# Attention, gating and mixing on one core: bank choice by longest free, and a fixed order for the first pair of heads

## The chip, the cores and the metric

The kernel runs on one core of one Trainium2 chip. The metric is the device time of one execution in microseconds (us); lower is better. A core has TensorE (PE, with its weight loads as PEld), VectorE (DVE), ScalarE (ACT), GpSimd (POOL) and SyncE (SP). SP and ACT both issue DMAs; their queues are written SPq and ACTq.

## The reference

Three blocks follow each other: attention over 4 x 12 heads of 448 tokens and 64 dimensions, a gated block with a spatial mix, and a token and channel mixer. Only the first touches the change:

```python
def rmsnorm(x, g):
    rms = np.sqrt(np.mean(x * x, axis=-1, keepdims=True) + 1e-06)
    return x / rms * g
q_n, k_n = (rmsnorm(q, g_q), rmsnorm(k, g_k))
scores = scale * np.matmul(q_n, k_n.transpose(0, 1, 3, 2))
scores = scores - np.max(scores, axis=-1, keepdims=True)
attn = np.exp(scores)
attn = attn / (np.sum(attn, axis=-1, keepdims=True) + 1e-09)
return np.matmul(attn, v).astype(np.float32)
```

The gated block computes relu(x w_in), splits it into u and v, normalises v, mixes it over tokens and multiplies; its weights, w_in among them, come as 8-byte floats and are converted word by word on the chip. The mixer is two more two-layer blocks, the last of which ("up" with products h2ps, "down" with products o_ps) is done as seven products of half-size blocks.

## The kernel before, in words

**Pairs.** Heads are worked in 24 pairs. `Attention.load` (line 634) brings q and k of a pair into one tile `raw` (two buffers); for pair 0 k's four pieces are issued by ACT, everything else by SP. `norms` (666) squares q and k on ACT, sums on DVE and calls `rsqrt` (605): Ln and Exp on ACT, with five small operations on POOL. `scale` (689) multiplies `raw` by the roots, on DVE for pair 0 and on POOL after it. `transposed` (699) turns q and k through PE into PSUM tiles `tp`, and copies them out as `qt` and `kt` (name `whole`); k's copy multiplies by the gain product `gg`. `scores` (728) makes the scores of one chunk of 112 tokens for both heads (tiles `sc`), their maxima on DVE (`nm`), and the exponentials on ACT (`e`). `turned` turns the exponentials (`et`), `values` multiplies by v (`av`).

**Start.** `start` (837) loads pair 0 and the gains, lets PE do 26 warm-up matmuls on zeros (`WARM`, 897), loads pair 1, and does norms, scaling and transposes of pair 0, and the norms of pair 1. After it, `slot` (863) yields one pair at a time, and other work is merged between: `prepare_v` (905) converts half of w_in through `convert` (540), whose first step is an Abs on ACT, then four bit operations on DVE (tile `word`), a copy on ACT and a difference on POOL (`wv`).

**Order.** Nothing is issued as the program is written. Every call goes into a `Plan` (150): each operation has a modelled cost (`estimate`, 217), dependencies and a weight. `place` (267) is a list scheduler: it keeps a clock for each engine, and always gives the engine that is free first its ready operation of least weight. Operations of POOL with SBUF operands and some of DVE's share a modelled port. `issue` (383) runs it forwards and backwards for eight rounds, the backward run giving the weights, and keeps the shortest plan. So each engine's instruction order is the plan's order of start times, and at run time an engine waits in that order.

**PSUM.** A PSUM tile is of kind sc, tp or mm. `Banks` (129) has eight banks, of which 4, 2 and 2 are reserved for the kinds. When `place` reaches the first operation of a tile, it picks one of the banks that are free at the planned time; before, the one that became free last:

```python
for k in ks:
    n = max(x for x in free_banks if x[0] <= t)
    free_banks.remove(n)
    bank[k] = n[1]
```

A bank's next writer waits at run time for the real last reader of the tile that had it.

Of the kernel before, what the change touches and what calls it, by code (L numbers as in the profile page):

```python
# [12 lines left out]
F32 = mybir.dt.float32  # L13
F32R = mybir.dt.float32r
U32 = mybir.dt.uint32
AF = mybir.ActivationFunctionType
# [133 lines left out]
class Plan:  # L150
# [116 lines left out]
    def place(self, before, after, lag, weight, tiles=None):  # L267
# [21 lines left out]
        while placed < len(ops):  # L289
# [35 lines left out]
            if tiles is not None and i in opens:  # L325
                ks = opens[i]
                kind = ks[0].psum
                spare = len(free_banks) - sum(max(0, n - held[x]) for x, n in Banks.OWN.items() if x != kind)
                if spare < len(ks):
                    blocked.append(i)  # L330
                    continue
                free_banks.sort()
                at = free_banks[len(ks) - 1][0]
                if at > t:
                    heapq.heappush(due[e], (at, i))
                    continue
                for k in ks:
                    n = max(x for x in free_banks if x[0] <= t)
                    free_banks.remove(n)
                    bank[k] = n[1]  # L340
                held[kind] += len(ks)
# [130 lines left out]
def attention_moe_mixer(  # L472
# [15 lines left out]
    C = 4  # L488
# [50 lines left out]

    def convert(pool, tag, bufs, raw, rows, n, dst_hi, dst_lo, dims=None, at=None):  # L540

        if f64:
            r = raw.rearrange("p (n w) -> p n w", w=2)
            a = pool.tile([rows, n], U32, tag=tag, bufs=bufs, name="word") if at is None else at
            low, high = r[:, :, 0], r[:, :, 1]
            nc.scalar.activation(a.bitcast(F32), high.bitcast(F32), AF.Abs)
            nc.vector.tensor_scalar(a.bitcast(F32), a.bitcast(F32), least, most, ALU.max, ALU.min)
            nc.vector.tensor_scalar(a, a, 5, 2, ALU.logical_shift_left, ALU.logical_shift_right)
            nc.vector.scalar_tensor_tensor(a, high, 0xC0000000, a, ALU.bitwise_and, ALU.bitwise_or)
            nc.vector.scalar_tensor_tensor(a, low, 29, a, ALU.logical_shift_right, ALU.bitwise_or)  # L550
        else:
            a = raw
# [51 lines left out]

    def rsqrt(pool, src, n, w, mul, tag, bufs=2, on=None):

# [3 lines left out]
        z = pool.tile([P, w], F32, tag=tag + "z", bufs=bufs, name=tag + "z")  # L610
        on.tensor_scalar(a[:n], src, mul, 1e-6, ALU.mult, ALU.add)
        nc.scalar.activation(y[:n], a[:n], AF.Ln)
        nc.scalar.activation(y[:n], y[:n], AF.Exp, scale=-0.5)
# [10 lines left out]
    class Attention:  # L624
# [9 lines left out]
        def load(self, i):  # L634
# [3 lines left out]
            t = self.p.tile([T, 2, C, 2, D], F32, tag="raw", bufs=2, name="raw")  # L638
            for r in range(2):
                nc.sync.dma_start(  # L640
                    out=t[:, 0, :, r], in_=q[b, 2 * j + r].rearrange("(c p) d -> p c d", p=T))
            on = nc.sync if i else nc.scalar
            on.dma_start(out=t[:, 1, :, 0], in_=k[b, 2 * j].rearrange("(c p) d -> p c d", p=T))

            src = k[b, 2 * j + 1]
            on.dma_start(out=t[:R, 1, 0, 1], in_=src[LAST:])
            on.dma_start(out=t[R:, 1, 0, 1], in_=src[:T - R])
            on.dma_start(
                out=t[:, 1, 1:, 1], in_=src[T - R:LAST].rearrange("(c p) d -> p c d", p=T))
            self.raw[i] = t  # L650
            if i == 2:
# [13 lines left out]

        def norms(self, i):
            if not 0 <= i < NP:
# [3 lines left out]
            ss = p.tile([P, n], F32, tag="ss", bufs=3, name="ss")  # L671
            self.r[i] = []
            for h in (slice(0, n // 2), slice(n // 2, n)):
                if i == 0 and h.start:
                    sq = p.tile([T, 2, S], F32, tag="e", bufs=EB, name="e").rearrange("p r s -> p (r s)")
                    sq = sq[:, :n // 2 * D].rearrange("p (n d) -> p n d", d=D)
                else:
                    sq = p.tile([T, n // 2, D], F32, tag="sq", bufs=1, name="sq")
                nc.scalar.activation(sq, raw[:, h], AF.Square)
                nc.vector.reduce_sum(ss[:T, h], sq, axis=AX.X)  # L680
                if i == 0:
                    self.r[i].append(rsqrt(
                        p, ss[:T, h], T, n // 2, 1.0 / D, f"r{h.start}", bufs=1,
                        on=nc.gpsimd))
            if i:
                r = rsqrt(p, ss[:T], T, n, 1.0 / D, "r", bufs=3, on=nc.gpsimd)
                self.r[i] = [r[:, :n // 2], r[:, n // 2:]]
# [10 lines left out]

        def transposed(self, i, a):
            if not 0 <= i < NP:  # L700
# [6 lines left out]
            if i < WHOLE:  # L707
                to = self.qt if a == 0 else self.kt
                t = to[i] = self.p.tile([P, S], F32, tag="qt" if a == 0 else "kt", name="whole")
                if i == 0 and a == 0:  # L710
                    nc.vector.tensor_copy(t, tpf)
                else:
                    nc.scalar.activation(t, tpf, AF.Copy, scale=1.0 if a == 0 else self.gg[:, 0:1])
                if a:
                    self.raw.pop(i), self.r.pop(i)
            elif a == 0:
# [11 lines left out]
        def scores(self, i, *cs):  # L728
# [108 lines left out]
        def start(self):  # L837
            self.load(0)
            g = self.p.tile([P, 2], F32, tag="g", bufs=1, name="g")
            for r in range(2):  # L840
                nc.sync.dma_start(out=g[r * D:(r + 1) * D, 0:1], in_=g_q.unsqueeze(1))
                nc.sync.dma_start(out=g[r * D:(r + 1) * D, 1:2], in_=g_k.unsqueeze(1))
            self.gg = self.p.tile([P, 1], F32, tag="gg", bufs=1, name="gg")
# [8 lines left out]
            tp = psum.tile([P, 512], "tp", "warm")  # L852
            zeros = self.rests[0].rearrange("p r d -> p (r d)")
            for _ in range(WARM):
                nc.tensor.matmul(tp[:, :P], zeros, zeros, start=True, stop=True)
# [40 lines left out]
    SLOT = 8  # L896
    WARM = 26
    TWO = 99
# [6 lines left out]
    def prepare_v(mp):  # L905
# [5 lines left out]
        for j in range(KD):  # L911

            wait = [op for _, op in at.third.writers] if j > 1 else ()
            raw = weights(mp, "vn", 4, wdram(w_in)[j * P:(j + 1) * P, DU * W:], P, (DU,), wait)
            convert(mp, "vr", 2, raw, P, DU, wv[:, HI, j], wv[:, LO, j])
            yield
# [575 lines left out]
```

## Time and profile before

| | |
|---|---|
| median of 3 runs | 887.33 us (885.97 to 889.61) |
| profiled execution | 887.2 us, its span 885.0 us |
| mean granted clock of PE | 0.995 |
| instructions | 15472 |
| DMA | 152.27 MB, mean 172 GB/s |

The span is what the trace covers; the 2.2 us beside it lie around it. Busy times are the union of an engine's instructions; DMA issues and waits count as idle. All times below count from the span's start. Nearly every instruction shows line 424, the planner's issuing line, so the groups are told apart by the tiles' names.

### The profile page before, as it was taken

What the parts mean: (1) busy time and instruction counts of PE and PEld (TensorE: products, weight loads), DVE (VectorE), ACT (ScalarE), POOL (GpSimd) and SP (SyncE); (2) the same over time, 40 slices, a digit from 0 to 9 for tenths busy, and PEclk for the clock granted to TensorE, in tenths of its full rate; (3) what the DMA queues carried; (4) which work ended last, traced back from release to release, by engine and by line L of the source; (5) the groups of instructions that cost most, each with busy time, mean ns of one, the idle gap of its engine ahead of it and who ended that gap; (6) DMA issues with size and microseconds to landing.
All of it is one profiled execution on the core that took longest, in us unless ns stands there. A gap on an engine that the chain in (4) does not pass through costs nothing.

```text
span 885.0 us, 15472 instructions
## 1 busy us (share of the span) xinstructions
PE 865.1 (98%) x5018; PEld 718.2 (81%) x5018; DVE 681.0 (77%) x1333; ACT 537.1 (61%) x1278; POOL 412.4 (47%) x541
## 2 busy tenths in 40 slices
PE   7999999999999999999999999999999999999998
PEld 5444567678777787776889999998989999999998
DVE  5799798987777767866366567889889886998973
ACT  5999988778867867866453356555325654343331
POOL 3555655786666646574234123224324108514560
PEclk8999999999999999999999999999999999999999
DMA  6555665566644575344687678776554745661441
GB/s 153 138 148 172 198 185 149 161 183 211 182 131 127 152 216 169 103 128 127 225 252 236 195 227 268 220 245 202 161 160 138 227 125 170 197 188 54 143 152 63
DMA packets 153263, 152.27 MB, mean 172 GB/s; under 512 B 77152, under 2 KB 136352, under 8 KB 153184
## 3 DMA queue, kind: packets, MB, share of 16 engines
q1 hardware_dynamic: 152224, 151.06, 57.2%
q8 instruction: 40, 0.66, 0.3%
q10 hardware_dynamic: 960, 0.23, 0.1%
q14 instruction: 39, 0.32, 0.1%
HBM read 112.44 MB, written 38.80 MB: 171 GB/s over the span
## 4 chain that ended last, share of the span: by engine, by line
PE 79%; DVE 8%; ACT 4%; issue 3%; DMA 3%; POOL 2%; SPq 1%; DVEq 0%; POOLq 0%; ACTq 0%
PE h2ps L424 15%; PE o_ps L424 15%; PE tp L424 9%; PE av L424 7%; PE sc L424 7%; PE vps L424 7%; PE xps L424 6%; PE ups L424 6%; PE sps L424 4%; PE h1ps L424 2%; PE u_ps L424 2%; DVE word L424 1%; DVE c L424 1%; DVE op L424 1%; DVE w L424 1%
## 5 line engine op out<-in xcount | busy, mean ns | idle before, releaser
L424 PE MATMUL h2ps<-op,w 128*128 128x448 f32 x756 | 155.5, 367 | 2.0 <-DVE c L424 2.0
L424 PE MATMUL o_ps<-w,op 128*128 128x384 f32 x882 | 153.6, 334 | 1.6 <-DVE u L424 1.6
L424 PEld LDWEIGHTS o_ps<-w,op 128*128 128x128 f32 x882 | 152.8, 188 | 2.3 <-ACT op L424 1.5
L424 PEld LDWEIGHTS h2ps<-op,w 128*128 128x128 f32 x756 | 141.3, 188 | 14.7 <-DVE c L424 3.7
L424 ACT ACTIVATE e<-sc,nm 112x448 f32<-112x448 f32 x192 | 122.5, 654 | 22.6 <-DVE nm L424 22.3
L424 DVE TENSOR_REDUCE nm<-sc 112x1 f32<-112x448 f32 x192 | 109.4, 614 | 19.6 <-PE sc L424 19.0
L424 POOL TENSOR_TENSOR src<-src 128x384 f32<-128x384 f32 x48 | 61.1, 1283 | 76.5 <-DMA src<-c_d 55.2
L424 ACT ACTIVATE op<-c 128x768 fp32r<-128x768 f32 x49 | 41.5, 847 | 85.5 <-PE o_ps L424 81.9
L424 PEld LDWEIGHTS tp<-ident,e 112*128 112x128 f32 x672 | 72.3, 140 | 24.3 <-ACT et L424 7.2
L424 POOL TENSOR_SCALAR e<-e,sums 112x448 f32<-112x448 f32 x112 | 73.8, 676 | 36.9 <-DVE sums L424 21.2
L424 PE MATMUL tp<-ident,e 112*128 112x112 f32 x672 | 87.1, 262 | 1.9 <-ACT over L424 1.5
L424 ACT ACTIVATE et<-tp 128x448 f32<-128x448 f32 x144 | 71.2, 527 | 18.2 <-PE tp L424 15.6
L424 DVE TENSOR_SCALAR word<-word 128x256 f32<-128x256 f32 (+5 forms) x132 | 57.9, 448 | 24.5 <-ACT word L424 23.4
L424 POOL TENSOR_TENSOR u<-u,o 128x384 f32<-128x384 f32 x28 | 40.3, 1457 | 69.2 <-ACT o L424 38.9
L424 DVE SCALAR_TENSOR_TENSOR word<-raw,word 128x256 uint32<-128x256 uint32 (+2 forms) x132 | 70.7, 541 | 1.3
L424 PE MATMUL ups<-xp,wu 128*128 128x448 f32 x288 | 67.8, 375 | 0.4 <-ACT et L424 0.4
L424 DVE TENSOR_TENSOR op<-c,op 128x768 fp32r<-128x768 f32 x49 | 58.1, 1185 | 10.3 <-ACT op L424 10.3
L424 PE MATMUL av<-et,v 128*64 128x448 f32 x288 | 61.2, 550 | 0.0
L424 DVE TENSOR_TENSOR c<-c,h2ps 128x448 f32<-128x448 f32 x84 | 50.1, 614 | 12.1 <-PE h2ps L424 11.9
L424 PE MATMUL vps<-wv,xp 128*128 128x512 f32 x216 | 59.3, 408 | 0.0
L424 PE MATMUL xps<-wo,g 128*128 128x384 f32 x288 | 58.2, 345 | 0.0
L424 PEld LDWEIGHTS ups<-xp,wu 128*128 128x128 f32 x288 | 52.2, 188 | 5.5 <-issue 1.0
(141 smaller groups left out, 1650.9 us busy)
## 6 DMA issues: line engine op xcount, KB each, us to landing
src<-c_d SPq DMA_DIRECT2D x132, 192.0 KB, 3.1
wu<-wu_d SPq DMA_DIRECT2D x16, 768.0 KB, 4.6
wo<-wo_d SPq DMA_DIRECT2D x16, 768.0 KB, 5.1
raw<-in_moe_w_ch_dram SPq DMA_DIRECT2D x36, 256.0 KB, 3.3
raw<-in_moe_w_ch_dram SPq DMA_DIRECT2D x24, 384.0 KB, 3.6
raw<-in_q_dram SPq DMA_DIRECT2D x48, 112.0 KB, 2.9
u<-u_d SPq DMA_DIRECT2D x28, 192.0 KB, 3.9
out_dram<-u SPq DMA_DIRECT2D x28, 192.0 KB, 1.9
```

The costliest lines, as they stand in the source:

```text
L424: getattr(getattr(self.nc, op.engine), fn)(*args, **kwargs)
```

## The change

It does five things. The bank taken is the one that has been free for longest. Pair 0's loads put k ahead of q: k's two large pieces and then q on SP, k's two small pieces and the gains on ACT. A new `first` takes the place of norms, scaling and transposes for pair 0: k is squared on ACT and its root done with DVE, k alone is scaled, q is squared on POOL and transposed unscaled, its copy is ACT's, and its root comes after k's copy. The exponentials of pair 0 take q's root as their scale, and POOL multiplies their maxima by it. The squares of pair 1 wait for k's scaling, and the first two conversions of w_in wait for the second function of q's root. The warm-up has 16 matmuls, and one more ahead of k's transposes.

```diff
-                    n = max(x for x in free_banks if x[0] <= t)
+                    n = min(x for x in free_banks if x[0] <= t)
...
-    def convert(pool, tag, bufs, raw, rows, n, dst_hi, dst_lo, dims=None, at=None):
+    def convert(pool, tag, bufs, raw, rows, n, dst_hi, dst_lo, dims=None, at=None, wait=()):
...
+            a.tile.after = list(a.tile.after) + list(wait)
             nc.scalar.activation(a.bitcast(F32), high.bitcast(F32), AF.Abs)
...
         on.tensor_scalar(a[:n], src, mul, 1e-6, ALU.mult, ALU.add)
+        y.tile.after = list(y.tile.after) + list(wait)
         nc.scalar.activation(y[:n], a[:n], AF.Ln)
...
+            both = nc.sync if i else nc.scalar
...
+            if i:
+                load_q(0, nc.sync)
+                load_q(1, nc.sync)
+            nc.sync.dma_start(out=t[:, 1, :, 0], in_=k[b, 2 * j].rearrange("(c p) d -> p c d", p=T))
...
+            both.dma_start(out=t[:R, 1, 0, 1], in_=src[LAST:])
+            both.dma_start(out=t[R:, 1, 0, 1], in_=src[:T - R])
+            nc.sync.dma_start(
                 out=t[:, 1, 1:, 1], in_=src[T - R:LAST].rearrange("(c p) d -> p c d", p=T))
+            if not i:
+                load_q(0, nc.sync)
+                load_q(1, nc.sync)
...
+                sq.tile.after = list(sq.tile.after) + list(wait)
                 nc.scalar.activation(sq, raw[:, h], AF.Square)
...
+        def first(self):
+            p, n = self.p, 2 * C
+            raw = self.raw[0].rearrange("p a c r d -> p a (c r) d")
+            self.r[0] = [None, None]
+
+            def squares(a, on):
+                sq = p.tile([T, 2, S], F32, tag="e", bufs=EB, name="e").rearrange("p r s -> p (r s)")
+                sq = sq[:, :n * D].rearrange("p (n d) -> p n d", d=D)
+                if on is nc.scalar:
+                    on.activation(sq, raw[:, a], AF.Square)
+                else:
+                    on.tensor_tensor(sq, raw[:, a], raw[:, a], op=ALU.mult)
+                return sq
+
+            def root(a, on, sq, behind=(), copied=()):
+                ss = p.tile([P, n], F32, tag=f"ss{a}", bufs=1, name="ss")
+                ss.tile.after = list(behind)
+                nc.vector.reduce_sum(ss[:T], sq, axis=AX.X)
+                self.r[0][a] = rsqrt(p, ss[:T], T, n, 1.0 / D, f"r{a}", bufs=1, on=on, wait=copied)
+                return nc.ops[-5]
+
+            sk = squares(1, nc.scalar)
+            sq = squares(0, nc.gpsimd)
+            known = root(1, nc.vector, sk)
+            self.scale(0)
+            scaled = nc.ops[-1]
+            self.scaled, self.known = scaled, known
+            self.transposed(0, 0, [known])
+            self.warm(WARM2, [op for _, op in self.qt[0].tile.writers])
+            self.transposed(0, 1)
+            return root(0, nc.gpsimd, sq, [scaled], [op for _, op in self.kt[0].tile.writers])
...
-            for a in range(2):
+            for a in range(2) if i else (1,):
                 on = nc.gpsimd if i else nc.vector
...
-                if i == 0 and a == 0:
-                    nc.vector.tensor_copy(t, tpf)
-                else:
-                    nc.scalar.activation(t, tpf, AF.Copy, scale=1.0 if a == 0 else self.gg[:, 0:1])
+                t.tile.after = list(t.tile.after) + list(wait)
+                nc.scalar.activation(t, tpf, AF.Copy, scale=1.0 if a == 0 else self.gg[:, 0:1])
...
+                roots = None
+                if i == 0:
+                    roots = self.r[0][0][:T]
+                    greatest, nm = nm, p.tile([P, 2], F32, tag="nm", bufs=4, name="nm")
+                    for r in range(2):
+                        at = 2 * c + r
+                        nc.gpsimd.tensor_tensor(
+                            nm[:T, r:r + 1], greatest[:T, r:r + 1], roots[:, at:at + 1], op=ALU.mult)
                 for r in range(2):
                     at = 2 * c + r
                     nc.scalar.activation(
-                        e[:, r], scs[c][r], AF.Exp, bias=nm[:T, r:r + 1], scale=1.0, accum_out=sums[:T, at:at + 1])
+                        e[:, r], scs[c][r], AF.Exp, bias=nm[:T, r:r + 1],
+                        scale=1.0 if i else roots[:, at:at + 1], accum_out=sums[:T, at:at + 1])
...
-                nc.sync.dma_start(out=g[r * D:(r + 1) * D, 0:1], in_=g_q.unsqueeze(1))
-                nc.sync.dma_start(out=g[r * D:(r + 1) * D, 1:2], in_=g_k.unsqueeze(1))
+                nc.scalar.dma_start(out=g[r * D:(r + 1) * D, 0:1], in_=g_q.unsqueeze(1))
+                nc.scalar.dma_start(out=g[r * D:(r + 1) * D, 1:2], in_=g_k.unsqueeze(1))
...
             self.load(1)
-            self.norms(0)
-            self.scale(0)
-            self.transposed(0, 0)
-            self.transposed(0, 1)
-            self.norms(1)
+            self.rooted = self.first()
+            self.norms(1, [self.scaled])
...
-    WARM = 26
+    WARM, WARM2 = 16, 1
...
+            behind = [] if wait else [at.rooted]
+            convert(mp, "vr", 2, raw, P, DU, wv[:, HI, j], wv[:, LO, j], wait=behind)
```

## Rows read from the trace of the kernel before

**Rows 1.** The page's busy times: engine, us (share of the span), instructions.
```profile
PE 865.1 (98%) x5018; PEld 718.2 (81%) x5018; DVE 681.0 (77%) x1333; ACT 537.1 (61%) x1278; POOL 412.4 (47%) x541
```
**Rows 2.** Stages: start:end length, busy us (instructions) per engine; PEclk granted, DMA share, GB/s.
```profile
0.73:14.47 13.74, 9.65 (x60) 9.03 (x60) 5.24 (x10) 6.04 (x13) 6.23 (x21) 0.96 0.71 169
14.47:20.20 5.73, 5.72 (x16) 2.50 (x18) 4.99 (x9) 3.72 (x11) 0.34 (x1) 0.50 0.68 173
20.20:90.00 69.80, 65.95 (x406) 33.74 (x403) 61.17 (x135) 69.09 (x196) 39.66 (x63) 1.00 0.55 152
90.00:523.50 433.50, 429.80 (x2617) 335.00 (x2616) 314.45 (x755) 295.26 (x785) 236.61 (x356) 1.00 0.60 176
523.50:548.60 25.10, 24.98 (x157) 24.07 (x156) 17.77 (x30) 16.91 (x34) 8.60 (x6) 1.00 0.84 250
548.60:882.00 333.40, 328.99 (x1768) 313.87 (x1768) 277.22 (x398) 146.11 (x244) 120.81 (x92) 1.00 0.54 166
```
**Rows 3.** The chain of waits in the head: start us, us, what.
```profile
7.80 5.41 DMA raw<-in_moe_w_in_dram
...
13.80 0.63 ACT whole L424
```
**Rows 4.** ACT's timeline: start us, us, operation, [idle before, released by].
```profile
6.03 0.63 ACT L424 ACTIVATE e<-raw 112x512 f32<-112x512 f32 x1 [1.42 <-DMA raw<-in_k_dram]
...
7.94 0.21 ACT L424 ACTIVATE r8y<-r8y 112x8 f32<-112x8 f32 x1
...
13.23 0.66 ACT L424 ACTIVATE word<-raw 128x512 f32<-128x512 f32 x1 [1.74 <-DMA raw<-in_moe_w_in_dram]
...
17.00 0.63 ACT L424 ACTIVATE e<-sc,nm 112x448 f32<-112x448 f32 x1 [1.64 <-DVE nm L424]
```
**Rows 5.** PE's timeline: k's transposes of pair 0, and scores at full clock.
```profile
10.99 0.60 PE L424 MATMUL tp<-ident,raw 112*128 112x112 f32 x4 [0.38 <-DVE gg L424]
...
22.85 1.01 PE L424 MATMUL sc<-whole 64*112 64x448 f32 x4
```
**Rows 6.** Timeline of the two issuing queues.
```profile
0.73 0.92 SPq L424 DMA_DIRECT2D raw<-in_q_dram  x2
...
3.38 0.33 ACTq L424 DMA_DIRECT2D raw<-in_k_dram  x1
```
**Rows 7.** DMA issues to 4.5 us: transfer, queue, count, size each, median us to landing.
```profile
raw<-in_k_dram ACTq DMA_DIRECT2D x1, 84.0 KB, 3.0
```
**Rows 8.** Tile views: durations in ns, min/median/max, first and last start in us, forms.
```profile
L424 SPq DMA_DIRECT2D g<-in_g_q_dram x2: 576/585/594, 1.7 to 6.5; - x2
...
L424 DVE TENSOR_TENSOR lrz<-lry x16: 147/153/691, 120.3 to 463.7; 128x1 f32<-128x1 f32 x16
```
**Rows 9.** Timeline of DVE and POOL.
```profile
6.69 0.69 DVE L424 TENSOR_REDUCE ss<-e 112x8 f32<-112x512 f32 x1 [1.37 <-ACT e L424]
...
9.95 0.20 POOL L424 TENSOR_TENSOR r8y<-r8y,r8z 112x8 f32<-112x8 f32 x1
...
10.25 0.68 DVE L424 TENSOR_TENSOR raw<-raw,r8y 112x512 f32<-112x512 f32 x1
...
12.77 2.04 POOL L424 TENSOR_TENSOR raw<-raw,ry 112x512 f32<-112x512 f32 x2
...
13.93 1.62 DVE L424 TENSOR_SCALAR word<-word 128x512 f32<-128x512 f32 x2 [2.40 <-ACT word L424]
...
16.34 1.16 DVE L424 TENSOR_REDUCE nm<-sc 112x1 f32<-112x448 f32 x2
...
18.91 0.42 DVE L424 TENSOR_SCALAR word<-word 128x512 f32<-128x512 f32 x1
...
28.39 1.26 POOL L424 TENSOR_TENSOR wv<-word,wv 128x512 fp32r<-128x512 f32 x1 [1.19 <-ACT wv L424]
```
**Rows 10.** Who PE waited for: us in total, times, longest us.
```profile
PE h2ps L424 <- DVE c L424: 2.0, 3, 0.7
...
PE o_ps L424 <- DVE u L424: 1.6, 2, 1.2
```

More of the change, by code (lines that the diff above doesn't have):

```diff
@@ L603, in mm_tile, with rsqrt @@
         return psum.tile([P, 512], "mm", name)
-    def rsqrt(pool, src, n, w, mul, tag, bufs=2, on=None):
+    def rsqrt(pool, src, n, w, mul, tag, bufs=2, on=None, wait=()):
         on = on or nc.vector
@@ L638, in load, with load_q @@
             t = self.p.tile([T, 2, C, 2, D], F32, tag="raw", bufs=2, name="raw")
-            for r in range(2):
-                nc.sync.dma_start(
+            both = nc.sync if i else nc.scalar
+            def load_q(r, on):
+                on.dma_start(
                     out=t[:, 0, :, r], in_=q[b, 2 * j + r].rearrange("(c p) d -> p c d", p=T))
-            on = nc.sync if i else nc.scalar
-            on.dma_start(out=t[:, 1, :, 0], in_=k[b, 2 * j].rearrange("(c p) d -> p c d", p=T))
+            if i:
+                load_q(0, nc.sync)
+                load_q(1, nc.sync)
+            nc.sync.dma_start(out=t[:, 1, :, 0], in_=k[b, 2 * j].rearrange("(c p) d -> p c d", p=T))
             src = k[b, 2 * j + 1]
-            on.dma_start(out=t[:R, 1, 0, 1], in_=src[LAST:])
-            on.dma_start(out=t[R:, 1, 0, 1], in_=src[:T - R])
-            on.dma_start(
+            both.dma_start(out=t[:R, 1, 0, 1], in_=src[LAST:])
+            both.dma_start(out=t[R:, 1, 0, 1], in_=src[:T - R])
+            nc.sync.dma_start(
                 out=t[:, 1, 1:, 1], in_=src[T - R:LAST].rearrange("(c p) d -> p c d", p=T))
+            if not i:
+                load_q(0, nc.sync)
+                load_q(1, nc.sync)
             self.raw[i] = t
@@ L664, in load_v, with norms @@
             self.v32[i] = t, rest
-        def norms(self, i):
+        def norms(self, i, wait=()):
             if not 0 <= i < NP:
@@ L671, in norms @@
             ss = p.tile([P, n], F32, tag="ss", bufs=3, name="ss")
-            self.r[i] = []
             for h in (slice(0, n // 2), slice(n // 2, n)):
-                if i == 0 and h.start:
-                    sq = p.tile([T, 2, S], F32, tag="e", bufs=EB, name="e").rearrange("p r s -> p (r s)")
-                    sq = sq[:, :n // 2 * D].rearrange("p (n d) -> p n d", d=D)
-                else:
-                    sq = p.tile([T, n // 2, D], F32, tag="sq", bufs=1, name="sq")
+                sq = p.tile([T, n // 2, D], F32, tag="sq", bufs=1, name="sq")
@@ L679, in norms @@
+                sq.tile.after = list(sq.tile.after) + list(wait)
                 nc.scalar.activation(sq, raw[:, h], AF.Square)
                 nc.vector.reduce_sum(ss[:T, h], sq, axis=AX.X)
[L681 to L687, printed above, removed]
+            r = rsqrt(p, ss[:T], T, n, 1.0 / D, "r", bufs=3, on=nc.gpsimd)
@@ new lines, in norms @@
+            self.r[i] = [r[:, :n // 2], r[:, n // 2:]]
+        def first(self):
[26 more added lines that the diff above has]
+            return root(0, nc.gpsimd, sq, [scaled], [op for _, op in self.kt[0].tile.writers])
@@ L689, in scale, with warm @@
+        def warm(self, n, wait=()):
+            tp = psum.tile([P, 512], "tp", "warm")
+            tp.tile.after = list(wait)
+            zeros = self.rests[0].rearrange("p r d -> p (r d)")
+            for _ in range(n):
+                nc.tensor.matmul(tp[:, :P], zeros, zeros, start=True, stop=True)
         def scale(self, i):
@@ L697, in scale, with transposed @@
                 on.tensor_tensor(raw, raw, roots.unsqueeze(2).to_broadcast([T, 2 * C, D]), op=ALU.mult)
-        def transposed(self, i, a):
+        def transposed(self, i, a, wait=()):
             if not 0 <= i < NP:
@@ L709, in transposed @@
                 t = to[i] = self.p.tile([P, S], F32, tag="qt" if a == 0 else "kt", name="whole")
-                if i == 0 and a == 0:
-                    nc.vector.tensor_copy(t, tpf)
-                else:
-                    nc.scalar.activation(t, tpf, AF.Copy, scale=1.0 if a == 0 else self.gg[:, 0:1])
+                t.tile.after = list(t.tile.after) + list(wait)
+                nc.scalar.activation(t, tpf, AF.Copy, scale=1.0 if a == 0 else self.gg[:, 0:1])
                 if a:
-                    self.raw.pop(i), self.r.pop(i)
+                    self.raw.pop(i)
+                    if i:
+                        self.r.pop(i)
             elif a == 0:
@@ L851, in start @@
                 self.rests.append(t)
[L852 to L855, printed above, removed]
+            self.warm(WARM)
             self.load(1)
-            self.norms(0)
-            self.scale(0)
-            self.transposed(0, 0)
-            self.transposed(0, 1)
-            self.norms(1)
+            self.rooted = self.first()
+            self.norms(1, [self.scaled])
         def slot(self, s):
@@ L914, in prepare_v @@
             raw = weights(mp, "vn", 4, wdram(w_in)[j * P:(j + 1) * P, DU * W:], P, (DU,), wait)
-            convert(mp, "vr", 2, raw, P, DU, wv[:, HI, j], wv[:, LO, j])
+            behind = [] if wait else [at.rooted]
+            convert(mp, "vr", 2, raw, P, DU, wv[:, HI, j], wv[:, LO, j], wait=behind)
             yield
```

## The prediction

> **What bounds the kernel now.** I read the page's busy shares first [rows 1]: PE is busy 98% of the span, so the time is PE's work plus the time in which PE has none. The table by stage [rows 2] says where that is. Of the 13.74 us ahead of the first scores PE is busy 9.65, and almost all of that is the warm-up, which computes nothing. From 14.47 to 20.20 PE is full, at a granted clock of 0.50, which is 1.2 GHz. From 20.2 to 90 ACT is busy 69.09 of 69.80 us and PE 65.95: here ACT leads. After that PE leads: 3.7 us without matmuls from 90 to 523.5, 0.1 in the next stage, 4.4 from 548.6 to 882. So two things can be won: the head, which delays ACT's full stretch and everything behind it one for one, and single PE waits, about 8 us in all behind 90.
>
> The chain of waits through the head [rows 3] runs over a load of w_in that lands 5.41 us after its issue at 7.80, and then over a copy of pair 0's k on ACT at 13.80. ACT's timeline [rows 4] shows why a weight load stands there: the conversion of w_in's first word sits ahead of the k copy in ACT's order and starts at 13.23, held by that load, although k's transposes were done at 11.59 [rows 5]. Scores start at 14.47, the first exponential at 17.00.
>
> **The change part by part.**
>
> *k's arrival.* Before, ACT squares k at 6.03, on k's landing; a last piece was issued on ACT's queue only at 3.38 [rows 4, 6]. Now k's two large pieces are SP's first issues, at 0.73 and about 1.19 (0.92 for two [rows 6]); 3.0 to land [rows 7] gives 4.2. The two small pieces and the four gain vectors are six issues on ACT's queue ahead of the square, 0.585 each [rows 8]: 0.77 + 3.5 = 4.3. Some issue may also be held, as the one at 3.38 seems to have been. I take 4.5, ends 4.2 and 5.2. That is 1.5 earlier.
>
> *k's root.* From the square's start to the end of the sum took 1.35 (6.03 to 6.69 + 0.69), and from there to the root's end, 9.95 + 0.20 on POOL, 2.77 [rows 4, 9]. Five POOL operations of 0.20 and two functions of 0.21 are 1.42 of that; the rest, seven hand-overs of 0.19, was lengthened by POOL doing both roots in turn. On DVE the five operations are 0.15 each [rows 8], the functions stay, and hand-overs of 0.1 (an estimate, half of before) make 1.8 in all. That puts the root at 4.5 + 1.35 + 1.8 = 7.65.
>
> But q's squares move to POOL. q is SP's third and fourth issue, at about 2.1, landing at 5.1; a two-operand POOL operation of 512 elements takes 1.26, so POOL reads until 6.4, while DVE is ready for the root at 5.85. The timeline shows what such a meeting does: two DVE operations took 1.62 beside POOL's scaling of 12.77 to 14.81, one alone 0.42 [rows 9]. I add 0.45, root at 8.1; ends 0 and 1.26. The Trainium skill ("SBUF — State Buffer", section "Who interferes with whom") has the same: whichever of the two engines issues first holds the shared pair of ports for its whole instruction and the other is blocked. By that rule the full 1.26 is lost when q lands just ahead of the root, and the head gains 0.8 less than I count; the trace agrees that DVE was stretched until POOL ended.
>
> *To the scores.* Scaling to transposes 0.74 (10.25 to 10.99 [rows 5, 9]), transposes 0.60, k copy 0.63 [rows 3, 5]: scores at 8.1 + 2.0 = 10.1 instead of 14.47, 4.35 earlier. q's copy, now ACT's (0.63 like k's), lies in the hole in which DVE does the root. The second pair's squares now wait for the scaling; behind them in ACT's order stands the k copy, and one square (0.63) just fits into the 1.34 of scaling and transposes. Without those holes each costs its length.
>
> *q's root, behind the scores.* Its sum waits for the scaling and takes 0.69, to 9.5; its two functions wait for the k copy, to 10.6; POOL's four operations at about 0.3 end at 11.8. Behind the sum on DVE stand the maxima: two heads' scores 1.01 at full clock [rows 5], one reduce 0.58 (1.16 for two [rows 9]), so 11.7; POOL's product 0.2 and a hand-over: first exponential at 12.1 against 17.00, 4.9 earlier. The eight POOL products are 0.2 each and hidden behind ACT's exponentials (0.63 each) once the stream runs; without that cover, 1.6.
>
> *w_in.* Its conversion now waits for q's root, but the planner may still put it ahead of the first exponentials. SP issues four gain vectors less (4 x 0.585) and two k pieces more (0.92): 1.4 earlier, so the word lands at 11.8. If ACT does its 0.66 first, the exponential starts at 12.5, 4.5 earlier. If DVE's word operations also stand ahead of the maxima (1.62 in before, and a hand-over), it starts at about 13.9, 3.1 earlier. I take **4.0 us** for the head, between the two and nearer to the first, as the trace shows the stall on ACT; ends 1.8 (the word lands no earlier than 13.21, and DVE waits for it too) and 5.7 (the 4.9, and 0.8 if PE keeps full clock).
>
> On that clock: PE had nothing from 11.59 on and was granted half clock behind it [rows 2, 5]. The new head has ten warm-up matmuls less and shorter holes; which of the two clocks the first scores get, no row tells, and half costs no more than before.
>
> Also moved: pair 2's load waits on SP for a buffer that k's transposes free, 2.1 earlier, and stands behind w_in as before.
>
> *Banks.* Taking the bank free for longest changes no planned start, since every candidate is free in the plan; it changes only how late the real reader may be. That excludes a loss but for noise. In the dense products PE waits three times, 2.0 us, for DVE's evictions of h2ps, and twice, 1.6, for those of o_ps [rows 10]; neither is data of the next product. I count these **3.6 us** as gone; what is late next is the next operand, made by the same DVE. Ends: 0, if they turn up there, and 5.9 (half of the other 4.5 behind 90 as well).
>
> **Sum.** 885.0 - 4.0 - 3.6 = 877.4 of span. The profiled execution took 887.2 for 885.0, 0.13 under the median of the runs, 887.33. So 877.4 + 2.2 + 0.1 = **879.7**.
>
> **The rivals.** About 0.5%, 4.4 us, is what can be told from no change: faster is under 882.9, slower over 891.8.
>
> *The banks do nothing*: the waits come back as waits for DVE's operands. For it: DVE is busy 277 of 333 us there, so it is DVE that is late. Against it: the waits are few and single, so DVE catches up. 883.3, the same by a hair.
>
> *w_in still holds the head*: ACT's and DVE's order puts the word ahead of the first exponentials, and SP's queue gains nothing. For it: ACT's stall of before is this very one. Against it: fewer issues on SP ahead of the load. Head 1.8: 881.9; with the banks doing nothing as well, 885.5. The change then doesn't do what it says: scores early, exponentials not.
>
> *The redrawn order uncovers the token stage* (slower). A new head makes the planner draw the whole order anew. From 523.5 to 548.6 PE is kept busy 24.98 of 25.10 us by what work is left over while tokens come in by DMA. If half that cover is spent earlier PE idles 12.5: 892.2. From 7.6 us of lost cover on the gain is gone. For it: the cover is the plan's doing, and the plan goes by modelled costs. Against it: the plan is picked for its length, and the stage shows almost no idle now.
>
> **How the numbers follow.** Forecast (head 3.1 to 5.7, banks 1.5 to 5.9): 0.53. Banks nothing: 0.19. w_in holds: 0.13, and both: 0.06. Token stage uncovered: 0.07. Beyond the good ends: 0.02. Faster takes the forecast less its weak corner (0.05), most of the w_in case (0.12) and the last: 0.62. Slower is the token stage, 0.07; the rest is 0.31. Low end: 885.0 - 5.7 - 5.9 + 2.3 = 875.7, set to 875.0 for what the redrawn order adds; high end 886.5, over both small cases together.
>
> **What the next profile would show.** Right: k's square near 4.5, scores near 10, the first exponential between 12 and 14, ACT full from some 4 us earlier, no PE wait of h2ps or o_ps on an eviction, a span near 877. Wrong: scores early, but ACT idle ahead of a word conversion; DVE's root stretched by more than 0.45 beside POOL's squares; new PE waits on op in the dense products; idle slices of PE around 520 to 550.

## The result, and the profile after

The changed kernel took 876.78 us in the median of 4 runs (876.03 to 879.06), beside 887.62 for the kernel before (885.97 to 889.61): a ratio of 0.9881, 95% interval 0.9854 to 0.9909. It is faster, by 10.8 us where 7.6 were forecast, and inside the range. Its profiled span is 874.6 us, 2.8 below the predicted 877.4.

The page's busy line, where [rows 1] had 865.1 for PE:

```profile
PE 858.5 (98%) x5000; PEld 719.0 (82%) x5000; DVE 679.9 (78%) x1336; ACT 536.4 (61%) x1278; POOL 426.0 (49%) x545
```

The share of 98% is the same, yet *busy* time fell by 6.6 us, although the only work that PE lost is nine matmuls of the warm-up, 1.9 us. Part of what went was stall inside busy time, as the groups below will show. The stages, to be read beside [rows 2] (length, then busy us and instructions of PE, PEld, DVE, ACT, POOL; granted clock, DMA share, GB/s):

```profile
0.73:10.78 10.05, 7.40 (x42) 7.00 (x42) 3.59 (x11) 4.08 (x9) 2.02 (x6) 1.00 0.69 152
10.78:20.20 9.42, 6.47 (x29) 3.46 (x30) 6.77 (x13) 8.73 (x23) 6.17 (x19) 0.82 0.72 193
20.20:90.00 69.80, 65.22 (x387) 33.50 (x385) 59.86 (x136) 67.48 (x190) 45.64 (x65) 0.98 0.58 158
90.00:523.50 433.50, 432.88 (x2657) 341.51 (x2656) 315.81 (x756) 296.62 (x789) 240.04 (x358) 1.00 0.60 178
523.50:548.60 25.10, 24.06 (x147) 22.92 (x146) 18.15 (x30) 15.29 (x29) 8.77 (x6) 1.00 0.84 275
548.60:871.00 322.40, 322.40 (x1746) 310.63 (x1744) 275.16 (x393) 144.24 (x242) 123.18 (x91) 1.00 0.54 167
```

Scores start at 10.78 instead of 14.47. From 90 to 523.5 PE is without matmuls for 0.6 us instead of 3.7, behind 548.6 for nothing at all instead of 4.4. What it still waits for stands ahead of 90, but for the last entry, in the token stage, and 0.6 us near 95 and 101 (us in total, times, longest):

```profile
PE tp L424 <- POOL raw L424: 2.9, 1, 2.9
PE av L424 <- ACT et L424: 2.7, 3, 1.9
PE tp L424 <- POOL wide L424: 1.8, 2, 1.0
...
PE h1ps L424 <- ACT xh L424: 0.9, 1, 0.9
```

Both entries of [rows 10] are gone. The head, on ACT's timeline beside [rows 4], then PE's beside [rows 5]:

```profile
5.31 0.63 ACT L424 ACTIVATE e<-raw 112x512 f32<-112x512 f32 x1 [3.29 <-DMA raw<-in_q_dram]
...
10.10 0.64 ACT L424 ACTIVATE whole<-tp,gg 128x448 f32<-128x448 f32 x1 [0.93 <-PE tp L424]
11.80 0.67 ACT L424 ACTIVATE word<-raw 128x512 f32<-128x512 f32 x1 [0.36 <-DMA raw<-in_moe_w_in_dram]
13.17 0.72 ACT L424 ACTIVATE e<-sc,nm,r0y 112x448 f32<-112x448 f32 x1
```

```profile
9.46 0.60 PE L424 MATMUL tp<-ident,raw 112*128 112x112 f32 x4 [1.15 <-DVE raw L424]
10.78 2.51 PE L424 MATMUL sc<-whole 64*112 64x448 f32 x12 [0.73 <-ACT whole L424]
16.24 0.65 PE L424 MATMUL tp<-ident,raw 112*128 112x112 f32 x4 [2.94 <-POOL raw L424]
16.82 1.83 PE L424 MATMUL sc<-whole 64*112 64x448 f32 x4
```

The first exponential comes 3.83 us earlier than before. Right behind it PE has a new hole of 2.94 us: pair 1's transposes wait for its scaling on POOL. Behind it the granted clock was half (0.50 from 18 to 20 us), as it was behind the hole of before: four matmuls of scores took 1.83 us, where [rows 5] has 1.01.

### The profile page after: what moved, and what is told of

Read it like the earlier page. It is cut to its first block, busy times and chain, and to the rows that moved or that the text cites. A ratio compares the mean times of both kernels' runs of the same rounds, so it can differ in the third digit from the quotient of the medians.

```text
span 874.6 us, 15410 instructions
## 1 busy us (share of the span) xinstructions
PE 858.5 (98%) x5000; PEld 719.0 (82%) x5000; DVE 679.9 (78%) x1336; ACT 536.4 (61%) x1278; POOL 426.0 (49%) x545
## 4 chain that ended last, share of the span: by engine, by line
PE 88%; DMA 3%; ACT 3%; DVE 2%; POOL 1%; issue 1%; SPq 1%; ACTq 0%; DVEq 0%; POOLq 0%
PE h2ps L424 18%; PE o_ps L424 17%; PE tp L424 9%; PE av L424 7%; PE vps L424 7%; PE xps L424 7%; PE ups L424 7%; PE sc L424 6%; PE sps L424 4%; PE h1ps L424 3%; PE u_ps L424 3%; DMA raw<-in_k_dram 2%; ACT e L424 1%; SPq L424 1%; DMA x<-x_d 1%
## 5 line engine op out<-in xcount | busy, mean ns | idle before, releaser
L424 PE MATMUL o_ps<-w,op 128*128 128x384 f32 x882 | 153.1, 334 | 0.0
L424 ACT ACTIVATE e<-sc,nm 112x448 f32<-112x448 f32 x184 | 118.4, 664 | 19.0 <-DVE nm L424 18.5
L424 POOL TENSOR_TENSOR src<-src 128x384 f32<-128x384 f32 x48 | 64.4, 1346 | 74.2 <-DMA src<-c_d 58.3
L424 PE MATMUL vps<-wv,xp 128*128 128x512 f32 x216 | 56.7, 404 | 0.0
```

Source lines behind the costliest of these rows:

```text
L424: getattr(getattr(self.nc, op.engine), fn)(*args, **kwargs)
```

## The experiments

Twelve runs. Ratios are to the kernel before, measured on the same chip beside each run (its median there 887.98 to 888.64).

### Bank choice and order taken apart

The kernel before with the new bank choice alone (in the two traces PE, ACT, DVE and POOL each do the same instructions in the same order), and the changed kernel with the old bank choice, in the changed kernel's order:

```diff
-                    n = max(x for x in free_banks if x[0] <= t)
+                    n = min(x for x in free_banks if x[0] <= t)
```

> The kernel before with the longest-free bank alone. Theory (banks and head are two separate gains): no PE wait of h2ps or o_ps on an eviction, the dense stages 5 to 6 us shorter, the head as before with scores at 14.5; 881 to 883. Rival A (the redrawn order did it all): 887, as before. Rival B (the banks did it all, the head's gain is lost on the way): 877.

877.88 us, ratio 0.9885 (0.9868 to 0.9903); span 876.0. That is below the theory's 881 to 883; the number is rival B's.

> The changed kernel with the bank that became free last, so the new head alone. Theory: scores near 10.8 and the first exponential near 13.2 as in the changed kernel, waits on evictions of h2ps and o_ps back; about 4 us under before, 882 to 884. Rival A (redrawn order): 877. Rival B (banks only): 887.

885.48 us, ratio 0.9966 (0.9956 to 0.9976); span 883.0. This lies between the theory's 882 to 884 and rival B's 887; the waits on evictions are back, but shorter than before (h2ps 0.9, o_ps 0.4). So the banks alone give nearly the whole gain, about 10 us, and head and new order alone 3. Together they don't quite add up: the changed kernel is 1.1 to 1.9 us under the first by the medians (its two measurements, here and below), 0.4 to 1.7 by the ratios, whose intervals overlap. So what the head adds on top of the banks isn't clear of the noise.

Where do 10 us come from, when the dense products showed only 3.6 of waits on evictions? The page's groups answer it (busy us, mean ns of one, idle just before them, and for whom). The kernel before:

```profile
L424 PE MATMUL h2ps<-op,w 128*128 128x448 f32 x756 | 155.5, 367 | 2.0 <-DVE c L424 2.0
L424 PE MATMUL o_ps<-w,op 128*128 128x384 f32 x882 | 153.6, 334 | 1.6 <-DVE u L424 1.6
L424 PE MATMUL tp<-ident,e 112*128 112x112 f32 x672 | 87.1, 262 | 1.9 <-ACT over L424 1.5 <-ACT whole L424 0.3
...
L424 PE MATMUL sps<-ws,vn 128*128 128x448 f32 x176 | 46.1, 381 | 0.9 <-ACT tg L424 0.8
```

and the same order with the new bank choice:

```profile
L424 PE MATMUL h2ps<-op,w 128*128 128x448 f32 x756 | 154.3, 366 | 0.0
L424 PE MATMUL o_ps<-w,op 128*128 128x384 f32 x882 | 153.1, 334 | 0.0
L424 PE MATMUL tp<-ident,e 112*128 112x112 f32 x672 | 86.3, 261 | 0.8 <-ACT over L424 0.6
...
L424 PE MATMUL sps<-ws,vn 128*128 128x448 f32 x176 | 46.2, 381 | 0.0
```

Add busy and idle: h2ps 157.5 to 154.3, o_ps 155.2 to 153.1. That is 5.3 us in the dense products, and 1.7 of it stood *inside* the busy time: the same matmuls were drawn out by the wait. The Trainium skill ("Perfetto Trace Analysis", its opening note) calls matmul busy time a bad metric, because matmuls are pipelined; that it misleads, these rows show, with 1.7 us of stall in it. The two spans differ by 9.0 us; the rest was won earlier: the first matmul of h2ps starts at 564.5 instead of 568.4. The transposes of exponentials give 1.9 of these 3.9 us and sps 0.8; other groups go both ways.

### Where along the kernel the bank choice pays

The changed kernel, with the new choice only behind 555 us of the plan, which is the dense products:

```diff
-                    n = min(x for x in free_banks if x[0] <= t)
+                    n = (min if t > 555000 else max)(x for x in free_banks if x[0] <= t)
```

> The changed kernel with the longest-free bank only from 555 us of planned time on, that is for the up and down stages, and the last-freed bank ahead of it. Theory (the bank's gain lies in the dense stages): within 1 us of the changed kernel, 877 to 878. Rival (its gain lies in the attention stretch, where many tiles turn over): 881 to 883, as the new head alone.

881.69 us, ratio 0.9925 (0.9909 to 0.9941): the theory missed, and the time is in the rival's range, though not that of the new head alone. Against the old choice throughout, 885.48, the dense products bring 3.8 us; the rest of the way to the changed kernel, 4.9 to 5.7 us, comes from ahead of them. By the two routes the dense products hold some four to six tenths of it.

### How far back a bank must be taken

The kernel before with the second-last freed bank, and with the third-last:

```diff
-                    n = max(x for x in free_banks if x[0] <= t)
+                    n = sorted(x for x in free_banks if x[0] <= t)[-2:][0]
```

> The kernel before with the bank that became free last but one, wherever two are free. Theory (PE waited because the real reader was late by a fraction of a tile's time, so one tile's turn of slack is nearly enough): 878 to 880, and no wait of h2ps or o_ps on an eviction. Rival (readers lag the plan by several tiles, so all eight banks are needed): 882 to 886.

881.1 us, ratio 0.9929 (0.9904 to 0.9953): between the two expectations.

> The kernel before with the third-last freed of the free banks taken (of fewer, the longest free), in the same order of instructions. Theory (a matmul stalls on an eviction only while a bank is given back too soon, and each place further back takes away stalls until none is left): the last freed cost 888, the second last 881.1, the longest free 877.9, so this one comes at 878 to 879.5, with no wait of h2ps or o_ps on an eviction in the trace. Rival (the gain of the longest free over the second last is chance of the execution, or comes from elsewhere than the evictions): about 881, as the second last.

879.6 us, ratio 0.9896 (0.9881 to 0.991). Neither has a PE wait of h2ps or o_ps left. So medians go 888, 881.1, 879.6, 877.9 from the last freed bank to the longest free: the first place back takes away about 7 us, the steps behind it 1.5 and 1.7. In the dense products the second-last gives all there is (h2ps 154.4 busy, o_ps 153.1, no idle time before either); what the longest free adds lies ahead of them, as h2ps starts at 565.9, 566.0 and 564.5 (one execution each). The first step is shown; the third-last isn't told apart from its neighbours with certainty, since its interval overlaps both of theirs.

### The word's wait alone

The kernel before, with the first two conversions of w_in made to wait for pair 0's k copy, so that the stall of [rows 3] goes. Nothing else is asked of the planner, but it draws a new order:

```diff
+            a.tile.after = list(a.tile.after) + list(wait)
...
+            behind = [] if wait else [op for _, op in at.kt[0].tile.writers]
```

> The kernel before with one thing of the new head: the first two conversions of w_in wait for pair 0's k copy. Theory (the k copy behind a late load was the larger half of the head): k copy at about 11.7 instead of 13.80, scores near 12.3, the time 1.5 to 2.5 us under before, 885 to 886. Rival (ACT is full behind it and the word only moves): scores earlier but the time as before, 887.

888.45 us, ratio 1.0009 (0.9995 to 1.0023): nothing, as the rival had it. The head did come forward (PE's and ACT's timelines):

```profile
12.47 3.32 PE L424 MATMUL sc<-whole 64*112 64x448 f32 x8 [0.72 <-ACT whole L424]
...
15.10 0.61 ACT L424 ACTIVATE e<-sc,nm 112x448 f32<-112x448 f32 x1
```

Scores come 2.0 and exponentials 1.9 us earlier. Pair 0 ends 1.1 earlier, but pair 2 0.5 later than before (a pair's end, here and below, is the start of ACT's copy of its result into `xp`, counted in order). An earlier first exponential isn't yet an earlier end.

### The changed kernel again, and its head made late

> The changed kernel once more, beside the others of this call. The bank choice alone took 877.9 (0.9885 of before) and the changed kernel 876.8 (0.9881), so the new head is worth 0.4 to 1.4 us on top of the banks: 0.986 to 0.989 of before, 876 to 878.5.

875.98 us, ratio 0.9866 (0.9846 to 0.9887); span 873.1. Its token stage (523.5 to 548.6) has PE busy 24.97 us, against 24.06 in the first profile.

Then the copy of pair 0's k is done eight times over, at the plan's cost of one, so that every engine's order stays:

```diff
-                nc.scalar.activation(t, tpf, AF.Copy, scale=1.0 if a == 0 else self.gg[:, 0:1])
+                with nc.joined_up():
+                    for n in range(8 if i == 0 and a else 1):
+                        nc.scalar.activation(t, tpf, AF.Copy, scale=1.0 if a == 0 else self.gg[:, 0:1])
+                        cost = cost if n else nc.ops[-1].cost
+                nc.ops[-1].cost = cost
```

> The changed kernel in its own order, with pair 0's k copy done eight times over (the seven more are not in the plan's costs), so that everything behind it starts about 3.6 us later: scores at 14.4 as in the kernel before. Theory (the head is worth its length, and the redrawn order gives back 2 to 3 us elsewhere): 3.2 to 3.8 us over the changed kernel, 880 to 880.6. Rival (ACT's and PE's stretch behind the head takes up the delay, so that an earlier start cannot gain much either): 1.5 us or less over it, 877 to 878.5.

881.58 us, ratio 0.9927 (0.991 to 0.9945). Scores start at 15.47, 4.67 later than in the repeat, not 3.6, as the eight copies took 5.30 us; the pairs run 4.7 later up to pair 3, 3.6 later from pair 6 to pair 23, and the end is 5.3 later in the span. Both expectations missed: by the medians it is 5.6 us over the repeat. With the order fixed, then, most of this lateness is not absorbed. Of the 1.7 us that come behind pair 23, 1.5 are one wait of PE for `xh` in the token stage, which the first profile of the changed kernel has with 0.9 and the repeat not at all. The 1.1 us that vanish between pairs 3 and 4 have a row. The values product of pair 4, in the repeat, and the granted clock behind it:

```profile
81.22 4.17 PE L424 MATMUL av<-et,v 128*64 128x448 f32 x12 [1.94 <-ACT et L424]
...
82.00:84.00 2.00, 2.00 (x7) 0.52 (x6) 2.00 (x5) 1.66 (x4) 0.28 (x1) 0.50 0.55 182
```

and with the late head:

```profile
85.97 2.48 PE L424 MATMUL av<-et,v 128*64 128x448 f32 x12 [1.95 <-ACT et L424]
...
86.00:88.00 2.00, 2.00 (x12) 0.83 (x14) 1.98 (x5) 1.60 (x4) 0.73 (x1) 1.00 0.44 140
```

The same hole of 1.95 us; behind one the granted clock was 0.50 (1.2 GHz), behind the other full (2.4 GHz). The half clock costs 1.7 us there.

### That clock held, and the longer warm-up

Six matmuls whose result is overwritten are put into the hole, the order kept:

```diff
+                    if i == 4 and kc == 0:
+                        for _ in range(6):
+                            nc.tensor.matmul(
+                                av[:D, :(C - 1) * D], v32[:, 0, 0], v32[:, 1].rearrange("p c d -> p (c d)"),
+                                start=True, stop=True)
+                        nc.joined[0].cost = 0
```

> The changed kernel, in the same order, with six matmuls on values that are long there, whose result is overwritten, put ahead of the values product of pair 4, where the PE stood idle for 1.9 us at 79.3 to 81.2 and the product behind it then ran at half clock in 4.17 us (2.48 in two other runs at full clock). Theory (the half clock behind that hole is where about 1.1 us of the earlier head is lost between pairs 3 and 4): the product takes about 2.5 us, pair 4 stands 1 to 1.7 us earlier, and the end comes 1 to 1.7 us earlier, at about 874.5 to 875.5. Rival (the stretch is paced by ACT there, so a faster PE only waits longer at the next exps): pair 4 and the end within 0.5 us of the changed kernel.

876.38 us, ratio 0.9856 (0.9838 to 0.9873). The product now runs at full clock (PE's timeline, the stretch, and PE's next idle time):

```profile
82.84 2.42 PE L424 MATMUL av<-et,v 128*64 128x448 f32 x11
...
101.16 0.57 PE L424 MATMUL tp<-ident,stage 112*128 112x112 f32 x4 [0.56 <-DMA stage<-in_moe_w_spatial_dram]
...
82.00:84.00 2.00, 2.00 (x15) 1.48 (x15) 2.00 (x5) 1.59 (x4) 0.73 (x1) 1.00 0.42 131
```

From pair 3 to pair 5 this run gained 1.5 us on the first profile (0.66 behind it, then 0.85 ahead). By pair 6 it was 0.2 behind again: part of what was won went to a load of the spatial weights (0.56). So the half clock is real, and no gain from its removal shows at the end: this execution was 0.7 late at pair 3 and 0.4 late in its span, and the runs can't tell a difference as small as that. The theory was right about the place, the rival about the time, though not about ACT as its cause.

```diff
-    WARM, WARM2 = 16, 1
+    WARM, WARM2 = 26, 1
```

> The changed kernel with 26 instead of 16 warm-up matmuls ahead of the first transposes (the prediction put ten fewer at nothing). Theory (the granted clock was full from the first of them and at the first transposes with 16 already): the same time within 1 us, scores within 0.6 us of 10.8, whatever the redrawn order adds or takes. Rival (the shorter warm-up leaves the clock less well held in the first 20 us, where it was half from 16.5 on): the half clock between 16 and 20 us goes, and the time falls by 1 us or more.

877.02 us, ratio 0.9866 (0.985 to 0.9883): no difference. The order is otherwise the changed kernel's. The half clock near 18 us stayed (four matmuls of scores at 18.45 took 1.84 us), so the rival falls. Its scores start at 12.06, 1.3 late because the extra matmuls stand ahead of k's transposes, twice the 0.6 that the theory allowed, and the pairs run 1.5 late up to pair 3. There it meets the same hole, and keeps its clock:

```profile
82.69 2.48 PE L424 MATMUL av<-et,v 128*64 128x448 f32 x12 [1.92 <-ACT et L424]
...
82.00:84.00 2.00, 1.31 (x8) 0.59 (x10) 1.94 (x6) 1.91 (x6) 0.73 (x1) 1.00 0.56 199
```

At pair 6 it is level with the changed kernel (0.04 us). A head 1.3 us later thus cost nothing, and one 4.7 us later most of its length. Why the clock falls behind one hole and not behind the other wasn't settled.

### Without the word's wait

The changed kernel without the wait of the first two conversions. The expectation below calls it a wait for k's scaling; in the kernel it is for the second function of q's root.

```diff
-            behind = [] if wait else [at.rooted]
+            behind = []
```

> The changed kernel without the wait that puts the first words of w_in behind the scaling of k: the first word's Abs then stands on ACT ahead of the two functions of q's root, and both words and one part ahead of the first exps. Theory (in the changed kernel w_in's pieces have landed by about 11.3 us, so words ahead of the root hold it until then and the first exps start 1 to 2 us later than 13.2; the PE is short of ACT's exps at the start of the attention, so the time is 877 to 878.5, by 1 to 2 us above the changed kernel's 876 to 876.8). Rival (the first exp waits for the scores and for the maxima anyway, and what ACT does ahead of them is lost in idle time): the same time as the changed kernel within 0.5 us.

883.99 us, ratio 0.9946 (0.993 to 0.9962), about 7 us above the changed kernel; both expectations missed. The first exponential came 1.2 us later, as the theory had it, but the order was drawn anew, and PE then stood for 5.6 us until POOL had scaled pair 1:

```profile
14.39 0.72 ACT L424 ACTIVATE e<-sc,nm,r0y 112x448 f32<-112x448 f32 x1 [0.16 <-POOL nm L424]
...
20.05 2.01 PE L424 MATMUL tp<-ident,raw 112*128 112x112 f32 x8 [5.57 <-POOL raw L424]
...
24.77 1.84 PE L424 MATMUL sc<-whole 64*112 64x448 f32 x4 [1.40 <-ACT whole L424]
```

Behind that hole the granted clock was 0.53 from 20.2 to 30 us, where the changed kernel had 1.00: again 1.84 us for four matmuls of scores. Pair 0 ends 4.9 us later, pairs 6 to 23 run 7 to 9.5 later. How the loss divides between the hole, the clock and the rest of the order isn't shown. This and the word's wait alone point the same way: what a dependency does to the drawn order can outweigh what it does to the stall.

### All of k on SP, q on ACT

```diff
-            both = nc.sync if i else nc.scalar
+            both = nc.sync
...
-                load_q(0, nc.sync)
-                load_q(1, nc.sync)
+                load_q(0, nc.scalar)
+                load_q(1, nc.scalar)
```

and the gain product `gg` is moved behind k's scaling on DVE.

> The changed kernel with all of k on SP's queue, q on ACT's ahead of the gains, and the product of the gains behind k's scaling on DVE. Theory of the head: k squared near 4.7 instead of 5.31 and the root not held by the gains, scores near 9.7 instead of 10.78. If the head is worth its length, 1 us under the changed kernel; if the stretch behind it takes it up, no difference; the planner draws a new order in any case, which can move it 2 us either way: 874 to 879.

874.29 us, ratio 0.9845 (0.9825 to 0.9864): its slowest run (874.37) is below the fastest of the repeat (875.29), so this beats both kernels. Not by its head, though: k's square starts at 6.06, scores at 11.14, later than the changed kernel's. Its order is drawn anew. It has no half clock from 79 to 90 (1.00 granted, 0.84 in the changed kernel), but more of it from 20.2 to 30 (0.79, where the changed kernel had 1.00), and it keeps PE busy 25.07 us in the token stage, as the repeat does with 24.97. The gain has to come from the order, as the head is later; what in the order gives it isn't shown.

## Why the prediction came out right

The direction came right for the reason given, that a bank free for longer spares waits. That the time fell inside the range was luck: two terms erred in opposite ways, banks with 3.6 predicted and about 10 measured, beyond their own upper end of 5.9, and the head with 4.0 predicted and 0.4 to 3.2 measured.

**Banks: the term that was mis-sized.** "Changes no planned start" held as far as the traces can tell, which have one order of instructions with either choice, and a loss was rightly excluded. The step that failed is "I count these 3.6 us as gone": I took the waits of [rows 10] for the whole cost. In the dense products it was 5.3, as a third of it lay in busy time; and ahead of them, where the middle value counted nothing and only the upper end of 5.9 took half of the idle time, there were some 4 to 6 more, part of them as PE's waits for ACT (`over`, `tg`). "What is late next is the next operand" didn't happen: no PE wait is left behind 548.6. The rival *the banks do nothing* falls.

**k's arrival**: 4.5 predicted, 5.31 measured, past the end of 5.2. The landing was not what held it. I had k's second piece at 1.19; the plan put two q pieces ahead of it, but it landed 2.6 us after 2.24, at about 4.85. ACT's own issues were the later of the two, as in my sum of 4.3, and two of them stood still (SP's queue, beside [rows 6], then ACT's):

```profile
0.74 0.39 SPq L424 DMA_DIRECT2D raw<-in_k_dram  x1
...
1.18 1.01 SPq L424 DMA_DIRECT2D raw<-in_q_dram  x2
...
2.24 0.49 SPq L424 DMA_DIRECT2D raw<-in_k_dram  x1
...
2.50 0.61 ACTq L424 DMA_DIRECT2D g<-in_g_k_dram  x1
...
4.00 0.47 ACTq L424 DMA_DIRECT2D g<-in_g_q_dram  x1
...
4.54 0.58 ACTq L424 DMA_DIRECT2D g<-in_g_k_dram  x1
```

The last issue ends at 5.12, and the square starts 0.19 later. In the repeat it is 5.33 and 5.51; with q on ACT, where all of k has landed by 5.44, it is 5.95 and 6.06. The two held issues start 0.02 us after the landings of q's first two pieces, which took 2.8 us each (1.18 to 3.98, 1.71 to 4.52); no row says why they should wait for these.

**k's root**: 3.6 from the square to its end predicted, 3.36 measured (8.50 + 0.17 - 5.31), but not by the meeting I priced. POOL's squares ran from 4.66 to 5.70, ahead of DVE's sum at 5.97, so the 0.45 was not lost. They took 1.04, like each of the two scalings in [rows 9]; I had taken 1.26 from the conversion there. Nor was the 1.26 by the Trainium skill's rule ("SBUF — State Buffer", section "Who interferes with whom"), since DVE and POOL did not meet there; no run here shows that meeting. In its place DVE waited for the gains, whose product stands in its order ahead of the root:

```profile
5.97 0.69 DVE L424 TENSOR_REDUCE ss<-e 112x8 f32<-112x512 f32 x1 [5.97 <-ACT e L424]
7.13 0.16 DVE L424 TENSOR_TENSOR gg<-g 128x1 f32<-128x1 f32 x1 [0.48 <-DMA raw<-in_k_dram]
7.21 0.17 DVE L424 TENSOR_SCALAR r1a<-ss 112x8 f32<-112x8 f32 x1
...
8.50 0.17 DVE L424 TENSOR_TENSOR r1y<-r1y,r1z 112x8 f32<-112x8 f32 x1
```

The row names k's load; what `gg` reads is the gains, the last of which ACT issued only at 4.54, and which landed 2.5 us later. Where the product was moved behind the scaling, in the run with q on ACT, the root follows the end of the sum by 0.03 us (7.41 to 7.44) instead of 0.56. A moved DMA has a reader too, and I followed only the queue.

**To the scores and the exponential**: 2.0 from root to scores (2.11 measured). From there 2.4 was predicted with the word ahead, and 2.39 measured. The word was ahead, and DVE's bit operations were not ahead of the maxima, but that the number fits is luck, as the word did not decide. The exponential at 13.17 follows POOL's product of the maxima, which ends at 13.13 (beside [rows 9]):

```profile
12.94 0.19 POOL L424 TENSOR_TENSOR nm<-nm,r0y 112x1 f32<-112x1 f32 x1
```

q's root came late: ACT put a square of pair 1 between its two functions, which ended at 11.44 instead of 10.6, and POOL put an operation of pair 1 among its own. In the late head the exponential (18.33) stands 0.03 us behind that product again, though ACT had been idle for half a microsecond. So the rival *w_in still holds the head* falls. The case with DVE's word operations ahead was also summed too short: 11.8, 0.66 and 1.62 make 14.1, and the maxima's 0.58 and the product's 0.2 come behind that, so the exponential would start near 14.9 and not at 13.9.

**What the head is worth: "one for one" failed.** 3.83 us at the first exponential, 2.73 at the end of pair 0, 0.84 at pair 2, 0.13 at pair 4. At pair 23 it is 4.2 again; against the run with the new bank choice alone the lead is 0.01 at pair 4 and 2.2 at pair 23. The two orders interleave the pairs differently, so one pair's mark alone says little. The step that broke is "hidden behind ACT's exponentials": POOL's eight products are hidden from ACT, but they and q's root stand in POOL's order among the work that pair 1 needs, and its scaling starts at 15.14 instead of 12.77 [rows 9]:

```profile
13.62 0.95 POOL L424 TENSOR_TENSOR nm<-nm,r0y 112x1 f32<-112x1 f32 x1
...
15.14 1.04 POOL L424 TENSOR_TENSOR raw<-raw,ry 112x512 f32<-112x512 f32 x1
...
19.99 1.54 POOL L424 TENSOR_TENSOR nm<-nm,r0y 112x1 f32<-112x1 f32 x1 [0.28 <-DVE nm L424]
```

Hence PE's hole of 2.94, and the half clock behind it. Products that take 0.19 elsewhere took 0.95 and 1.54, and each ended about 0.05 us behind a bit operation of DVE on the word (14.57 and 14.52, 21.52 and 21.48). The exponentials of pair 0 also grew from 0.63 to 0.72, eight times, which I hadn't priced. The half clock at pair 4 (1.7) is the third part, though holding the clock didn't move the end. What each part costs no run shows by itself, and not all of the rest need be loss: ACT was busy 1.4 us more by 90. In the end the head and its order are worth 3.2 us without the new bank choice, and 0.4 to 1.9 on top of it, which isn't clear of the noise.

**The warm-up**: ten matmuls less cost nothing. The first scores had the full clock (twelve matmuls in 2.51 us), which I had counted only in the upper end, and ten matmuls more changed no time. **The token stage**: uncovered by 0.9 us in one execution and not in the next, nowhere near 7.6; the slower rival falls for this order, while the run without the word's wait shows that a redrawn order can cost 7.

## What to carry to other kernels

Where buffers rotate under a plan made ahead of time, take the one that has been free for longest: it costs nothing in the plan and gives every late reader its slack, and the visible waits on it were a lower bound here, so add busy and idle of a group before pricing them. Price an earlier start only as far as the next engine in the chain follows: look up what that engine has queued ahead of the second unit of work, not only of the first. A DMA issue given to an engine is also work in that engine's own order: here ACT's square had to stand behind its loads of the gains. And with a scheduler that redraws everything, one added dependency should be timed by itself, since here its side effects ranged from nothing to 7 us.

## What the runs showed of the hardware

An exponential with a scale per row took 0.72 us, with a constant scale 0.63, both with a bias per row. The Trainium skill ("ScalarE: Activation LUTs", section "What ACT_TABLE_LOAD costs") gives about 93 ns for each per-partition pointer operand; the rows agree (0.09). Holes of PE of nearly one length (1.92 to 1.95 us) were followed by half clock in two executions of the changed kernel and by full clock with the late head and with the longer warm-up.

The granted clock of a row can miss half speed at the start. The changed kernel's trace has 1.00 throughout the warm-up, yet its matmuls start 0.21 us apart up to about 6.3 us and 0.11 apart behind it, though PE is busy all the time:

```profile
4.00:5.00 1.00, 1.00 (x7) 1.00 (x6) 0.00 (x0) 0.00 (x0) 0.34 (x1) 1.00 0.56 118
...
7.00:8.00 1.00, 1.00 (x12) 1.00 (x11) 0.45 (x4) 0.42 (x2) 0.00 (x0) 1.00 0.58 94
```

So the expectation of the longer warm-up, that the clock was full from the first matmul, holds for the granted clock shown and not for the matmuls; with 16 of them the full rate was there ahead of the first transposes at 7.52.
